# Attention in pairs of steps: both scores, both sets of transposes, then two weighted-value products in a row

## The chip, the cores and the metric

The kernel runs on one core of one Trainium2 chip. What counts is the device time of one execution in microseconds (us), and runs of the kernel are compared by their median. The engines are PE (TensorE: matrix products and transposes), DVE (VectorE), ACT (ScalarE), POOL (GpSimd) and SP (SyncE, which issues the DMAs). In the rows, PEld stands for the loads of PE's weights, which run beside its products.

## The reference

Clustered attention, then two expert layers on its output. Only the attention is touched by the change.

```python
def _attn_ref(q, k, v, centroids):            # (2, 8, 768, 64), 16 centroids a head
    ...
    q_assign = np.argmax(np.einsum('bhsd,hcd->bhsc', q_n, c_n), axis=-1)
    k_assign = np.argmax(np.einsum('bhsd,hcd->bhsc', k_n, c_n), axis=-1)
    mask = q_assign[:, :, :, None] == k_assign[:, :, None, :]
    scores = scale * np.matmul(q, k.transpose(0, 1, 3, 2))
    scores = np.where(mask, scores, -1000000000.0)
    scores = scores - np.max(scores, axis=-1, keepdims=True)
    attn = np.exp(scores)
    attn = attn / (np.sum(attn, axis=-1, keepdims=True) + 1e-09)
    return np.matmul(attn, v).astype(np.float32)

def reference(**kwargs):
    ...
    x = np.ascontiguousarray(attn_out.transpose(0, 2, 1, 3)).reshape(B * S, H * D)
    x = _moe_ref(x=x, **moe_kwargs)           # x @ w_in, a rational function, @ w_out
    return _moe2_ref(x=x, **moe2_kwargs)      # silu(x @ w_gate) * (x @ w_val) @ w_out
```

## The kernel before

Attention works on head pairs: 2 batches of 4 pairs of heads, 8 in all. A head pair has two halves of 384 queries; a half has three blocks of 128 queries for each of its two heads. One block of one head is a **step**, so a half has 6 steps (`PER`), a head pair 12, and the whole stage 96 (`order`). `n` counts the steps.

A step passes through these functions:

- `scores` (L344, L346): four products into `s_ps`, 128 queries by 768 keys, in PSUM. The centroid mask is part of the second product. `s_ps` has 2 buffers.
- `maximum` (L354): DVE takes the row maxima, into `st`.
- `exponentials` (L362): ACT makes `p` and the row sums. `p` has 3 buffers.
- `transposes` (L400), `LAG` = 2 steps later: PE transposes the six 128x128 blocks of `p` in two groups of three, each into a tile `t_ps`; each tile is copied to `pt` by ACT (L405), or in the second group of the steps in `dve_evac` by DVE (L403). The pool of `t_ps` has 3 buffers, which `r_ps` and `sim` share.
- `weighted` (L411): one of the six key blocks of a half that is finished: for each head one product of `v` and `pt`, summed up in `o_ps`, which has one buffer. The six are queued in `pv` once a half's last transposes stand in the program.

Each half also needs the reciprocals of its row sums: `reciprocals` (L369, L372, DVE), `spread` (L377: PE transposes them into `r_ps`; L379: ACT copies them; L381: a DMA to DRAM), `bring_back` (L388: a DMA back, broadcast over partitions into `rb`). When the sixth `weighted` of a half is there, `normalised` (L419, DVE) multiplies `o_ps` by `rb`, and `split_x` (L433, L434, POOL) splits the result for the expert layers.

`background` places other work between the steps: for the next head pair the centroid products `sims` (L277, PE), the search for the nearest centroid on DVE (`to_tokens` L284, `largest` L298, `reached` L303, `weigh` L309, `first_reached` L312, `one_hot` L315, `mask_values` L321, `to_rows` L329), and the split of the heads' q and k on POOL (L249 to L268); from step 60 on also nine weight blocks for the expert layers (L70 on ACT, L79 and L83 on DVE, L89 and L94 on POOL).

The order is written by hand: every engine runs its own instructions in the order in which the Python code makes them, and waits at the head of its queue for what an instruction needs. The loop from L540 on sets it, one step at a time:

```python
    for n in range(len(order) + LAG):
        s = n % (2 * PER)
        if n < len(order):
            scores(*order[n])
            maximum(*order[n])
```

After the loop `tail` does the last half's `weighted` in the first two rounds of the expert layers.

Of the kernel before, what the change touches and what calls it, by code (L numbers as in the profile page):

```python
# [20 lines left out]
def tile_kernel(ctx, tc, q_t, k_t, q_s, k_s, v_l, cent, w_in, w_out, a_co, b_co, w_gate, w_val, w_o2, out):  # L21
# [128 lines left out]
    order = [(b, hp, half, i, e) for b, hp in pairs for half in range(2) for i in range(HB) for e in range(2)]  # L150
    PER = 2 * HB
# [186 lines left out]
    def scores(b, hp, half, i, e):  # L338
        t = heads[b, 2 * hp + e]
        s_ps = ps_s.tile([P, S], F32, tag="s", name="s_ps")  # L340
        q0 = half * HALF + i * P
        qs = slice(q0, q0 + P)
        for lo, hi in CUT:
            nc.tensor.matmul(s_ps[:, lo:hi], t["q1"][:, qs], t["k1"][:, lo:hi], start=True, stop=False)  # L344
        for lo, hi in CUT:
            nc.tensor.matmul(s_ps[:, lo:hi], t["q2"][0:KM, qs], t["k2"][0:KM, lo:hi], start=False, stop=True)  # L346
        if (i, e) == (0, 0):
            live["st", b, hp, half] = st_p.tile([P, 3, PER], F32, tag="st", name="st")
        live["s", b, hp, half, i, e] = s_ps

    def maximum(b, hp, half, i, e):
        st = live["st", b, hp, half]
        k = e * HB + i
        nc.vector.tensor_reduce(  # L354
            out=st[:, 0, k:k + 1], in_=live["s", b, hp, half, i, e], axis=AX.X, op=ALU.max, negate=True
        )
# [33 lines left out]
    def transposes(b, hp, half, i, e, on_dve):  # L390
        p = live.pop(("p", b, hp, half, i, e))
        if i == 0:
            live["pt", b, hp, half, e] = pt_p.tile([P, NB, HALF], F32, tag="pt", name="pt")
        pt = live["pt", b, hp, half, e]
        qc = slice(i * P, (i + 1) * P)
        for g in range(2):
            t_ps = t_tile("t_ps")
            for j in range(HB):
                kb = g * HB + j
                nc.tensor.transpose(t_ps[:, j, :], p[:, kb * P:(kb + 1) * P], ident)  # L400
            ks = slice(g * HB, (g + 1) * HB)
            if g == 1 and on_dve:
                nc.vector.tensor_copy(out=pt[:, ks, qc], in_=t_ps)  # L403
            else:
                nc.scalar.copy(out=pt[:, ks, qc], in_=t_ps)  # L405
# [77 lines left out]
    dve_evac = (2, 8, 10, 11)  # L483
    n_early, every = 9, 4
    early0 = 60
    XS, BB = 3, 4
# [50 lines left out]
                    load_qk(b, 2 * hp + 1)  # L537

    LAG = 2
    for n in range(len(order) + LAG):  # L540
        s = n % (2 * PER)
        if n < len(order):
            scores(*order[n])
            maximum(*order[n])
        finished = None
        if pv:
            step = pv.pop(0)
            weighted(*step)
            if step[3] == NB - 1:
                finished = step[:3]  # L550
        if n >= LAG:
            transposes(*order[n - LAG], s in dve_evac)
        if n < len(order):
            exponentials(*order[n])
        if n % PER == 0 and n:
            reciprocals(*order[n - 1][:3])
        if n % PER == 1 and n > 1:
            spread(*order[n - 2][:3])
        if n % PER == BB and n > PER:
            bring_back(*order[n - BB - 1][:3])  # L560
        for engine in ("dma", "pe", "dve", "pool", "act"):
            background(n, engine)
        if finished:
            normalised(*finished)
            split_x(*finished)
        if n >= LAG and (n - LAG) % PER == PER - 1:
            pv.extend([order[n - LAG][:3] + (kb,) for kb in range(NB)])
# [269 lines left out]
```

## Time and profile before

| | us |
|---|---|
| median of 3 runs | 844.63 |
| lowest and highest | 844.25, 846.31 |
| the profiled execution | 844.0 |
| its span, from first to last instruction | 842.2 |

The rows further down come from one profiled execution. Their times start at the first instruction; each row of a timeline merges neighbouring instructions of one kind. `idle before <-releaser` in square brackets is how long the engine had been idle and what ended that; "issue" is idle time for which the profile shows no wait. The ends of matrix products are modelled, so starts are read here. Attention is the first 260 us of the span, the expert layers are the rest.

### The profile page before, as it was taken

Reading aid. Unit: us, or ns where it says so; the run is one execution under the profiler, and the core shown is the slowest. Engines: PE = TensorE matmul, PEld = TensorE weight load, DVE = VectorE, ACT = ScalarE, POOL = GpSimd, SP = SyncE. Lnnn points to the kernel's source line nnn. Section 1 sums busy time; section 2 is a strip of 40 time slices with the busy share of each in tenths; the row PEclk is TensorE's granted clock in tenths of the full one; section 3 lists DMA queues with packets and bytes.
Section 4 is the critical chain, followed back from the end, with each engine's and each line's share of the span. In section 5 each row is a group of like instructions: output and inputs, shape, how many; then the busy total and the mean of one; then the engine's idle time right before and its main releaser. Section 6 shows DMA issues by size and latency. Waiting matters only on the chain.

```text
span 842.2 us, 11048 instructions
## 1 busy us (share of the span) xinstructions
PE 807.8 (96%) x3900; PEld 606.0 (72%) x3900; DVE 621.3 (74%) x929; ACT 450.1 (53%) x850; POOL 311.9 (37%) x274
## 2 busy tenths in 40 slices
PE   4999999999899999999999989999999999999998
PEld 3665566555466887777777767788888888888886
DVE  7776687677765999999999999985576555434435
ACT  5666776666486897667667666842432222211111
POOL 3566375465532333433333433321244323211112
PEclk8899999999899999999999999999999999999999
DMA  5255335435222211111111211122223121100004
GB/s 179 83 174 168 112 87 169 148 117 172 76 87 90 75 51 59 68 50 51 51 50 55 72 50 51 51 75 76 75 90 104 57 75 50 51 26 1 0 1 149
DMA packets 26550, 67.90 MB, mean 81 GB/s; under 512 B 4448, under 2 KB 9536, under 8 KB 26496
## 3 DMA queue, kind: packets, MB, share of 16 engines
q1 hardware_dynamic: 26496, 67.21, 24.4%
q8 instruction: 30, 0.49, 0.2%
q14 instruction: 24, 0.20, 0.1%
HBM read 59.48 MB, written 3.19 MB: 74 GB/s over the span
## 4 chain that ended last, share of the span: by engine, by line
PE 70%; DVE 22%; issue 3%; ACT 2%; POOL 1%; DMA 1%; SPq 0%; DVEq 0%; POOLq 0%; ACTq 0%
PE h_ps L601 29%; PE acc L677 17%; PE o_ps L411 8%; PE t_ps L400 8%; PE s_ps L344 4%; PE s_ps L346 3%; DVE g L634 3%; DVE part L695 3%; DVE td L640 3%; DVE td L637 2%; DVE tq L620 2%; DVE tp L623 2%; DVE c L79 1%; DVE c L83 1%; DVE st L354 1%
## 5 line engine op out<-in xcount | busy, mean ns | idle before, releaser
L601 PE MATMUL h_ps<-yhl,w 128*128 128x512 f32 x864 | 201.8, 389 | 0.0
L601 PEld LDWEIGHTS h_ps<-yhl,w 128*128 128x128 f32 x864 | 162.2, 188 | 33.7
L677 PE MATMUL acc<-g,w 128*128 128x512 f32 x576 | 144.9, 395 | 11.5 <-DVE part L695 6.8
L601 PE MATMUL h_ps<-xhl,w 128*128 128x512 f32 x576 | 138.8, 390 | 0.0
L677 PEld LDWEIGHTS acc<-g,w 128*128 128x128 f32 x576 | 106.2, 188 | 42.2 <-DVE part L695 10.8
L94 POOL TENSOR_TENSOR w<-c,w 128x512 fp32r<-128x512 f32 x68 | 92.9, 1368 | 108.5 <-ACT w L91 101.4
L601 PEld LDWEIGHTS h_ps<-xhl,w 128*128 128x128 f32 x576 | 107.9, 188 | 23.9 <-issue 1.2
L645 POOL TENSOR_TENSOR g<-td,tr 128x512 fp32r<-128x512 f32 x46 | 59.6, 1295 | 172.7 <-DVE td L640 151.8
L354 DVE TENSOR_REDUCE st<-s_ps 128x1 f32<-128x768 f32 x96 | 91.3, 952 | 32.1 <-PE s_ps L346 29.3
L405 ACT COPY pt<-t_ps 128x384 f32<-128x384 f32 x160 | 70.4, 482 | 68.7 <-PE t_ps L400 68.5
L695 DVE TENSOR_TENSOR part<-acc,part 128x512 f32<-128x512 f32 x74 | 48.6, 685 | 75.3 <-PE acc L677 75.2
L400 PEld LDWEIGHTS t_ps<-ident,p 128*128 128x128 f32 x576 | 63.5, 144 | 55.7 <-issue 42.1
L677 PE MATMUL acc<-w,g 128*128 128x512 f32 x432 | 103.3, 389 | 0.0
L362 ACT ACTIVATE p<-s_ps,st 128x768 f32<-128x768 f32 x96 | 87.5, 912 | 11.3 <-DVE st L354 8.1
L677 PEld LDWEIGHTS acc<-w,g 128*128 128x128 f32 x432 | 81.1, 188 | 16.8
L411 PE MATMUL o_ps<-pt,v 128*64 128x384 f32 x384 | 84.1, 519 | 3.6 <-DVE x L419 3.6
L400 PE MATMUL t_ps<-ident,p 128*128 128x128 f32 x576 | 86.0, 287 | 0.0
L692 ACT COPY ts<-acc 128x512 f32<-128x512 f32 x22 | 12.9, 588 | 111.4 <-PE acc L677 111.4
L693 POOL TENSOR_TENSOR part<-ts,part 128x512 f32<-128x512 f32 x22 | 30.3, 1394 | 111.9 <-ACT ts L692 111.8
L618 ACT ACTIVATE tq<-h_ps,babs 128x512 f32<-128x512 f32 x48 | 33.0, 688 | 68.9 <-PE h_ps L601 66.6
L344 PE MATMUL s_ps<-k,q 128*128 128x512 f32 x192 | 59.7, 393 | 2.8 <-ACT p L362 2.7
L83 DVE SCALAR_TENSOR_TENSOR c<-raw,c 128x512 uint32<-128x512 uint32 x68 | 57.2, 841 | 2.0
(101 smaller groups left out, 1049.4 us busy)
## 6 DMA issues: line engine op xcount, KB each, us to landing
raw<-w_in_dram SPq DMA_DIRECT2D x16, 512.0 KB, 3.6
raw<-w_out_dram SPq DMA_DIRECT2D x16, 512.0 KB, 3.3
raw<-w_gate_dram SPq DMA_DIRECT2D x12, 512.0 KB, 3.3
raw<-w_val_dram SPq DMA_DIRECT2D x12, 512.0 KB, 3.3
raw<-w_o_dram SPq DMA_DIRECT2D x12, 512.0 KB, 3.3
xq<-q_t_dram SPq DMA_DIRECT2D x14, 384.0 KB, 4.6
xk<-k_t_dram SPq DMA_DIRECT2D x14, 384.0 KB, 6.4
sq<-q_s_dram SPq DMA_DIRECT2D x8, 384.0 KB, 3.0
```

The costliest lines, as they stand in the source:

```text
L83: nc.vector.scalar_tensor_tensor(out=cb, in0=t["low"].bitcast(U32), scalar=29, in1=cb, op0=ALU.logical_shift_right, op1=ALU.bitwise_or)
L94: nc.gpsimd.tensor_tensor(out=w[:, 1, :], in0=t["c"], in1=r32(w[:, 0, :]), op=ALU.subtract)
L344: nc.tensor.matmul(s_ps[:, lo:hi], t["q1"][:, qs], t["k1"][:, lo:hi], start=True, stop=False)
L354: nc.vector.tensor_reduce(out=st[:, 0, k:k + 1], in_=live["s", b, hp, half, i, e], axis=AX.X, op=ALU.max, negate=True)
L362: nc.scalar.activation(out=p, in_=live.pop(("s", b, hp, half, i, e)), func=AF.Exp, bias=st[:, 0, k:k + 1], accum_out=st[:, 1, k:k + 1],)
L400: nc.tensor.transpose(t_ps[:, j, :], p[:, kb * P:(kb + 1) * P], ident)
L405: nc.scalar.copy(out=pt[:, ks, qc], in_=t_ps)
L411: nc.tensor.matmul(live["o", b, hp, half][e * D:(e + 1) * D, :], heads[b, 2 * hp + e]["v"][:, kb, :], live["pt", b, hp, half, e][:, kb, :] ...
L601: nc.tensor.matmul(h_ps, w[:, wi, cs], x[:, xi, cc, :], start=(n == 0), stop=(n == 3 * NCC - 1))
L645: spread.tensor_tensor(out=g[:, 1, :], in0=td, in1=tr, op=ALU.mult)
L677: nc.tensor.matmul(acc[c], lhs, rhs, start=(first and m == 0), stop=(last and m == 2))
L695: nc.vector.tensor_tensor(out=pt[:, c, :], in0=banks[c], in1=pt[:, c, :], op=ALU.add)
```

## The change

The loop takes two steps at a time. In a pair it emits both `scores` and both `maximum`, the transposes of the first of the two steps that are due, both `exponentials`, the transposes of the second, then (where a half has ended) `reciprocals` and `spread` together, then two `weighted` in a row, then the background of both steps. `spread` used to stand in the step after `reciprocals`. The buffers, `LAG`, the copies' engines and the queue `pv` are as before.

```diff
     LAG = 2
-    for n in range(len(order) + LAG):
-        s = n % (2 * PER)
-        if n < len(order):
-            scores(*order[n])
-            maximum(*order[n])
-        finished = None
+    def next_weighted():
         if pv:
             step = pv.pop(0)
             weighted(*step)
             if step[3] == NB - 1:
-                finished = step[:3]
-        if n >= LAG:
-            transposes(*order[n - LAG], s in dve_evac)
-        if n < len(order):
-            exponentials(*order[n])
-        if n % PER == 0 and n:
-            reciprocals(*order[n - 1][:3])
-        if n % PER == 1 and n > 1:
-            spread(*order[n - 2][:3])
-        if n % PER == BB and n > PER:
-            bring_back(*order[n - BB - 1][:3])
-        for engine in ("dma", "pe", "dve", "pool", "act"):
-            background(n, engine)
+                return step[:3]
+
+
+    for n0 in range(0, len(order) + LAG, 2):
+        for n in (n0, n0 + 1):
+            if n < len(order):
+                scores(*order[n])
+                maximum(*order[n])
+        m0, m1 = n0 < len(order), n0 >= LAG
+        if m1:
+            transposes(*order[n0 - LAG], n0 % (2 * PER) in dve_evac)
+        if m0:
+            exponentials(*order[n0])
+            exponentials(*order[n0 + 1])
+        if m1:
+            transposes(*order[n0 + 1 - LAG], (n0 + 1) % (2 * PER) in dve_evac)
+        if n0 % PER == 0 and n0:
+            reciprocals(*order[n0 - 1][:3])
+            spread(*order[n0 - 1][:3])
+        finished = next_weighted()
+        finished = next_weighted() or finished
+        for n in (n0, n0 + 1):
+            if n % PER == BB and n > PER:
+                bring_back(*order[n - BB - 1][:3])
+            for engine in ("dma", "pe", "dve", "pool", "act"):
+                background(n, engine)
         if finished:
             normalised(*finished)
             split_x(*finished)
```

On PE, two steps in the middle of a half stand like this in the kernel before (one row for each group of like instructions; k and q have the numbers of the two heads):

```order
L344 MATMUL s_ps<-k_294,q_292 128x512
L344 MATMUL s_ps<-k_294,q_292 128x256
L346 MATMUL s_ps<-k_295,q_293 128x512
L346 MATMUL s_ps<-k_295,q_293 128x256
L411 MATMUL o_ps<-pt,v 64x384 x2
L400 MATMUL t_ps<-ident,p 128x128 x6
L344 MATMUL s_ps<-k_383,q_381 128x512
L344 MATMUL s_ps<-k_383,q_381 128x256
L346 MATMUL s_ps<-k_384,q_382 128x512
L346 MATMUL s_ps<-k_384,q_382 128x256
L411 MATMUL o_ps<-pt,v 64x384 x2
L400 MATMUL t_ps<-ident,p 128x128 x6
```

And like this in the changed kernel:

```order
L344 MATMUL s_ps<-k_302,q_300 128x512
L344 MATMUL s_ps<-k_302,q_300 128x256
L346 MATMUL s_ps<-k_303,q_301 128x512
L346 MATMUL s_ps<-k_303,q_301 128x256
L344 MATMUL s_ps<-k_401,q_399 128x512
L344 MATMUL s_ps<-k_401,q_399 128x256
L346 MATMUL s_ps<-k_402,q_400 128x512
L346 MATMUL s_ps<-k_402,q_400 128x256
L400 MATMUL t_ps<-ident,p 128x128 x12
L411 MATMUL o_ps<-pt,v 64x384 x4
```

The same instructions stand there; each kind is now in one block of twice the length, and the weighted products come last.

On DVE, around the middle of a head pair, from the maxima of steps 4 and 5 to those of step 7 and `normalised`, before:

```order
L354 TENSOR_REDUCE st<-s_ps 128x1
L312 TENSOR_REDUCE mx<-sm 128x24
L354 TENSOR_REDUCE st<-s_ps 128x1
L315 TENSOR_TENSOR sm<-wt,mx 128x384
L321 TENSOR_SCALAR sm<-sm,msk 128x384
L354 TENSOR_REDUCE st<-s_ps 128x1
L369 TENSOR_SCALAR st<-st 128x6
L372 RECIPROCAL st<-st 128x6
L329 STREAM_TRANSPOSE t_768<-sm 128x384
L354 TENSOR_REDUCE st<-s_ps 128x1
L419 TENSOR_TENSOR x<-o_ps,rb 128x384
```

And in the changed kernel:

```order
L354 TENSOR_REDUCE st<-s_ps 128x1 x2
L312 TENSOR_REDUCE mx<-sm 128x24
L315 TENSOR_TENSOR sm<-wt,mx 128x384
L321 TENSOR_SCALAR sm<-sm,msk 128x384
L354 TENSOR_REDUCE st<-s_ps 128x1 x2
L369 TENSOR_SCALAR st<-st 128x6
L372 RECIPROCAL st<-st 128x6
L329 STREAM_TRANSPOSE t_794<-sm 128x384
L419 TENSOR_TENSOR x<-o_ps,rb 128x384
```

The maxima stand in twos, the background work of both steps between them, and the reciprocals (L369, L372) stand behind two maxima instead of one.

On PE, where a half ends and a new head pair begins, before (the transpose of the reciprocals, L377, follows one step later, behind that step's transposes):

```order
L411 MATMUL o_ps<-pt,v 64x384 x2
L400 MATMUL t_ps<-ident,p 128x128 x6
L277 MATMUL sim<-sq,ct 32x384 x2
L277 MATMUL sim<-sk,ct 32x384 x2
L344 MATMUL s_ps<-k_717,q_715 128x512
```

And in the changed kernel:

```order
L400 MATMUL t_ps<-ident,p 128x128 x12
L377 MATMUL r_ps<-ident,st 6x128
L411 MATMUL o_ps<-pt,v 64x384 x4
L277 MATMUL sim<-sq,ct 32x384 x2
L277 MATMUL sim<-sk,ct 32x384 x2
L344 MATMUL s_ps<-k_626,q_624 128x512
```

L377 now stands in the same pair as the reciprocals and ahead of its weighted products, and the centroid products stand behind these instead of behind the transposes.

## Rows read from the trace of the kernel before

**Rows 1.** Stretch, length; busy us (count) PE, PEld, DVE, ACT, POOL; PE clock, DMA, GB/s.

```profile
45.97:74.95 28.98, 28.98 (x182) 17.34 (x178) 21.37 (x30) 19.83 (x47) 17.10 (x17) 1.00 0.51 166
...
132.70:161.56 28.86, 28.86 (x182) 17.32 (x178) 20.46 (x30) 19.74 (x47) 16.95 (x17) 1.00 0.48 155
161.56:195.66 34.10, 31.07 (x183) 18.42 (x179) 26.44 (x36) 21.63 (x50) 21.43 (x22) 0.95 0.39 124
195.66:231.47 35.81, 31.04 (x175) 18.43 (x171) 27.41 (x36) 20.55 (x48) 22.25 (x22) 0.90 0.38 122
```

**Rows 2.** Timeline of weight loads (PEld), one quiet step; columns: start, length, what.

```profile
84.27 0.30 PEld L344 LDWEIGHTS s_ps<-k,q 128*128 128x128 f32 x2
...
85.18 0.20 PEld L411 LDWEIGHTS o_ps<-pt,v 128*64 128x64 f32 x4 [0.25 <-issue]
85.97 0.64 PEld L400 LDWEIGHTS t_ps<-ident,p 128*128 128x128 f32 x6 [0.60 <-issue]
86.58 0.30 PEld L344 LDWEIGHTS s_ps<-k,q 128*128 128x128 f32 x2
```

**Rows 3.** Timeline of weight loads, three weighted products in a row in the tail.

```profile
263.32 0.20 PEld L411 LDWEIGHTS o_ps<-pt,v 128*64 128x64 f32 x4 [0.35 <-issue]
...
265.41 0.76 PEld L601 LDWEIGHTS h_ps<-xhl,w 128*128 128x128 f32 x4 [0.60 <-issue]
```

**Rows 4.** Timeline of weight loads, first head pair, steps without weighted products.

```profile
27.72 0.30 PEld L344 LDWEIGHTS s_ps<-k,q 128*128 128x128 f32 x2 [0.33 <-ACT p L362]
...
28.41 0.70 PEld L400 LDWEIGHTS t_ps<-ident,p 128*128 128x128 f32 x6
...
29.36 0.30 PEld L344 LDWEIGHTS s_ps<-k,q 128*128 128x128 f32 x2 [0.25 <-ACT p L362]
```

**Rows 5.** Timeline of weight loads, transposes with centroid products behind them.

```profile
102.23 0.64 PEld L400 LDWEIGHTS t_ps<-ident,p 128*128 128x128 f32 x6 [0.60 <-issue]
103.03 0.11 PEld L277 LDWEIGHTS sim<-sq,ct 128*32 128x32 f32 x2 [0.17 <-DVE st L372]
```

**Rows 6.** Timeline of the other engines in the step of rows 2, and later.

```profile
84.25 0.86 ACT L405 COPY pt<-t_ps 128x384 f32<-128x384 f32 x2 [0.55 <-PE t_ps L400]
...
85.00 0.92 ACT L362 ACTIVATE p<-s_ps,st 128x768 f32<-128x768 f32 x1
...
85.28 0.96 DVE L354 TENSOR_REDUCE st<-s_ps 128x1 f32<-128x768 f32 x1 [0.87 <-PE s_ps L346]
...
86.56 0.86 ACT L405 COPY pt<-t_ps 128x384 f32<-128x384 f32 x2 [0.55 <-PE t_ps L400]
...
205.94 0.19 ACT L362 ACTIVATION_READ_ACCUMULATOR p<-s_ps,st 128x1 f32 x1
...
206.18 0.30 PEld L344 LDWEIGHTS s_ps<-k,q 128*128 128x128 f32 x2 [1.18 <-ACT p L362]
```

**Rows 7.** The reciprocals: timelines at two places, then line L369 in sum (ns).

```profile
32.44 0.19 DVE L372 RECIPROCAL st<-st 128x6 f32<-128x6 f32 x1
...
32.74 0.08 PEld L377 LDWEIGHTS r_ps<-ident,st 128*6 128x6 f32 x1 [0.35 <-issue]
...
87.83 0.94 DVE L354 TENSOR_REDUCE st<-s_ps 128x1 f32<-128x768 f32 x1
88.69 0.93 DVE L369 TENSOR_SCALAR st<-st 128x6 f32<-128x6 f32 x1
...
L369 DVE TENSOR_SCALAR st<-st x16: 154/160/939, 32.2 to 258.4; 128x6 f32<-128x6 f32 x16
```

**Rows 8.** Timeline of PE near the start, transposes that keep it at work.

```profile
7.20 3.93 PE L198 MATMUL w_ps<-ident 128*128 128x128 f32 x27
```

**Rows 9.** Busy time by stretch, columns as in rows 1, where the clock differs.

```profile
8.79:12.00 3.21, 2.69 (x23) 2.37 (x21) 3.21 (x7) 2.01 (x4) 2.75 (x2) 1.00 0.27 61
...
212.50:217.00 4.50, 1.83 (x13) 1.26 (x11) 4.46 (x7) 1.74 (x4) 3.71 (x4) 1.00 0.20 44
217.00:223.83 6.83, 5.67 (x18) 2.88 (x18) 3.79 (x6) 3.06 (x7) 4.52 (x5) 0.50 0.37 108
```

## Prediction

> **What bounds the kernel now.** The change touches only the attention stage, which ends at about 260 us; the expert layers behind it keep their code, and I count them as unchanged. I first cut that stage by head pair, that is by 12 steps, from the score of step 12k+1 to the same score of the next head pair, with the view of busy time by stretches [rows 1]. Four head pairs take 28.86 to 28.98 us each (the first and the last of them are shown); PE is busy for all of that time at clock 1.00, DVE for about 21 us and ACT for 20. So PE sets the end there. The next two (34.10 and 35.81 us) are different: DVE has 26 to 27 us of work, PE is idle for 3 and 5 us, and the mean clock is below 1.
>
> Then I read one step on PE by its weight loads, since a load starts when PE turns to the next kind of work [rows 2]. Call the four score products S, the six transposes T and the two weighted-value products W. S lasts 0.91 us until W loads, W 0.79 until T loads, T 0.61 until the next S: 2.31 a step, 4.62 for two. The reader is to see the idle time with no releaser ("issue") before W and before T, which S behind T does not have: these are turns of PE, not waits.
>
> **The change part by part.**
>
> *Fewer turns of PE.* What each kind lasts when its own kind follows can be read elsewhere in the trace. S with T behind it lasts 0.69 [rows 4]. Three W in a row, in the tail, last 2.09, so (2.09 - 0.79) / 2 = 0.65 for a W with a W behind it [rows 3]. A T that comes after S spreads its six loads over 0.70 instead of 0.64, so it lasts 0.67 [rows 2, 4]. T with a differently shaped product behind it lasts 0.80 instead of 0.61, so 0.19 more [rows 5]. The new pair S S T T W W is then 0.69 + 0.69 + 0.67 + 0.67 + 0.19 + 0.65 + 0.79 = 4.35 us. Against 4.62 that saves 0.27 a pair, some 12 us over the 44 pairs that have W, if PE never waits.
>
> *A fourth transpose tile.* A pair writes four t_ps tiles and the pool has three, so the fourth waits for the copy of the first. Count from the pair's first S load: the T loads begin at 1.38. From T's first load to the first copy a step takes 0.59 [rows 2, 6], 0.65 with the slower loads; the copy takes 0.48, and PE goes on 0.05 after ACT is done (205.94 + 0.19 to 206.18) [rows 6]. The tile is free at 1.38 + 0.65 + 0.48 + 0.05 = 2.56. PE wants it one and a half T later, at 1.38 + 0.67 + 0.33 = 2.38. So 0.18 is lost, and a pair is 4.53. No row shows this wait itself. Its bounds are 0 (the copy ends in time) and 0.5 (one more copy of ACT ahead of it); I take 0.18, because each part of it has a row. That leaves 0.09 saved a pair.
>
> *ACT and the score buffers.* ACT copies the first two tiles from 2.03 on (the two take 0.75), then does both exponentials at 2.78 and 3.70 (0.92 each), then two more copies at 4.62 [rows 6]. The score buffers come free some 0.14 after an exponential's end, at 3.84 and 4.76; the next pair wants them at 4.53 and 5.22. So both waits are hidden by about 0.5, and DVE's maxima may start about 1.3 late before PE feels it. If that cover goes, each further us of lateness is one on PE.
>
> *The reciprocals, moved next to their transpose.* Before, DVE did L369 and L372 in one step and PE transposed the result (L377) at the end of the next one. Now both stand in the pair that starts a half, and L377 stands ahead of W W on PE. The first maximum starts 1.00 after S's load [rows 2, 6], the second 0.86 later, L369 0.86 after that [rows 7], at 2.72, L372 0.20 later; it ends at 3.11, and PE loads L377 0.11 after that [rows 7], at 3.22. PE is there at 2.89. So 0.33 is lost, twice a head pair; L377 itself costs 0.1 as before. With the turn and W W such a pair is 4.89. L369 also has two lengths, 0.16 and 0.93 [rows 7]; four of its 16 were long, all in the middle of a head pair, where GpSimd prepares the next heads. That was covered by a step; now 0.77 would go straight onto PE. It hit four of the seven middles that have such GpSimd work: 0.44 a head pair.
>
> *The centroid products (sims)* move behind W W, where they wait for the third copy (4.62 + 0.48 + 0.05 = 5.15 against 4.89) but save the turn behind T (0.19). They took 28.9 - 12 x 2.31 - 2 x 0.1 = 0.98 and I leave them at that. DVE stands idle with to_tokens at the head of its queue until they are done, so the maxima of the next pair start about 0.6 late, which is within the 1.3. The normalised product, which L411 waited for in the busy head pairs, gets a whole pair more time.
>
> *The sum.* A quiet head pair: 4 x 4.53 + 2 x 4.89 + 0.98 + 0.44 = 29.3 against 28.9, so 0.4 slower; I add 0.15 for lateness that DVE carries into the middle pair. Four of them: +2.2. In the first head pair W is missing and the pair goes round the chain S, T, copies, two exponentials: 0.69 + 0.65 + 0.75 + 1.84 + 0.2 = 4.13 against two steps of 1.64 [rows 4]: +0.85, for the one pair that this holds. The last 12 steps have no preparation for a next head: -0.1.
>
> *The two busy head pairs* also prepare weight blocks on DVE. I walked DVE through them with the lengths that its operations had there before. In the first three pairs of each it has 5 to 6 us of work for a pair of 4.5, and in the first of them it idles for sims. By the middle pair its maxima are some 3 us late; 1.3 of that is covered, and then L377 waits for all that is left. This makes 4.4 and 5.6 us of delay, and behind waits of that length PE falls to half its clock for a stretch [rows 9], which I put at 1.1 us each. After: 2 x 28.86 + 4.4 + 5.6 + 2.2 = 69.9. Before: 34.10 + 35.81 [rows 1] and the 0.98 of the sims that stand just ahead, 70.9. So -1.0, with 3 us either way.
>
> Total: 0.85 + 2.2 - 1.0 - 0.1 = +2.0 us. The profiled execution took 844.0 (span 842.2), so 846.0. It lies 0.6 below the median of the runs shown (844.63), and I forecast 846.5.
>
> **The rivals.** *PE's saving survives (faster).* If the fourth tile's wait is near its lower bound and L369 stays short, a quiet head pair is 4 x 4.35 + 2 x 4.89 + 0.98 = 28.2, 0.7 faster; over six head pairs that is -4. If the busy ones, which stand 12 us above two quiet ones [rows 1], lose a third of that too, it is -8: 837 to 841. For it: PE is the bound, and every term of the saving has a row. Against it: each new wait is worked out from rows as well.
>
> *DVE's lateness lands on L377 (slower).* In the middle pair of a head pair L377 waits for everything that DVE still has to do. If L369 is long there and the operations before it too, since they share their cause, DVE is 1 to 2 us late in the quiet head pairs also. It decides from a lateness of 0.2 on, as nothing covers L377 any more. At 1 us for each of the six or seven, and one more stretch at half clock (2 us), the time is 846.5 + 8 to 9, so 852 to 856. For it: the 0.93 row. Against it: DVE is busy for only 21 of 29 us there [rows 1].
>
> *The clock falls among the transposes (slower).* In rows 9 PE fell to half its clock (1.2 GHz) behind a stretch in which it was busy for 1.83 of 4.50 us. The new pair has 12 transposes and a wait in a row, about 1.7 of 4.5 us. If that made it fall once in each half, for half the 6.83 us of rows 9, of which about half is lost, 15 halves are some 25 us: 870. Against it: at the start PE did 27 transposes in a row [rows 8], and the clock behind their first part was 1.00 [rows 9]. The Trainium skill's page "TensorE: Matmul & The Clock Gate" (Part 4) says that transposes do not count as busy for the clock as other matmuls do; by that rule the fall would come. The trace speaks mostly against it here.
>
> **How the numbers follow.** Forecast 0.43 (846.5, by itself 843 to 850), saving survives 0.27, DVE onto L377 0.26, clock 0.04. About 0.3% (2.5 us, so 842.1 to 847.2 is "the same") is what a measurement of this kernel can tell from no change. The forecast's case gives 0.03 faster, 0.28 same, 0.12 slower; the first rival 0.23 faster and 0.04 same; the second 0.02 same and 0.24 slower; the clock 0.04 slower. Faster 0.26, same 0.34, slower 0.40. The range takes in the upper part of the fast rival and most of the slow one: 839.5 to 855.
>
> **What would show it.** In the new profile PE's loads in a quiet pair should read 0.69 and 0.69 for the scores, then 12 transposes with an idle time of about 0.2 before the tenth that ACT's copy ends, then W W in 1.44; pairs should start 4.5 apart. L377 should wait for L372 by 0.3, or by 1.1 where L369 is long. If pairs are 4.35 apart, the tile term was wrong; if L377 does not wait, the reciprocal term was. I am wrong altogether if PE waits for ACT's exponentials in quiet pairs, or if the two busy head pairs move by more than 3 us.

## The result, and the profile after

The changed kernel took **854.49 us** (median of 4 runs, 852.39 to 855.76) against 844.44 for the kernel before beside it (4 runs): a ratio of **1.0117**, 95% interval 1.0084 to 1.015. It is about 10 us slower. The time lies near the upper end of the range, and where the second rival, "DVE's lateness lands on L377", put it (852 to 856), not at the forecast of 846.5. The profiled execution of the changed kernel took 855.41, its span 853.6, 11.4 more than the span before.

First the busy time by head pair, cut at the first score load of each head pair's first step. The columns are the stretch, its length, busy time of PE, weight loads, DVE, ACT and POOL, granted clock, DMA share and GB/s, as in [rows 1]. The kernel before, cut the same way: a quiet head pair and the two busy ones.

```profile
100.53:129.41 28.88, 28.88 (x180) 17.34 (x179) 21.84 (x30) 19.73 (x47) 16.28 (x16) 1.00 0.43 132
158.27:192.37 34.10, 31.07 (x181) 18.42 (x180) 26.42 (x36) 21.63 (x50) 20.72 (x22) 0.95 0.40 134
192.37:229.13 36.76, 31.99 (x180) 18.59 (x179) 27.40 (x37) 21.50 (x50) 22.24 (x23) 0.91 0.40 124
```

The changed kernel, the same three head pairs and the stretch at half clock in the first busy one:

```profile
104.46:134.87 30.41, 28.44 (x180) 18.53 (x178) 21.56 (x30) 19.31 (x47) 16.27 (x16) 1.00 0.41 124
165.28:202.29 37.01, 31.68 (x180) 20.02 (x178) 24.56 (x36) 20.95 (x50) 20.44 (x20) 0.91 0.39 126
202.29:239.96 37.67, 31.30 (x180) 19.91 (x178) 26.29 (x37) 21.14 (x50) 22.13 (x22) 0.91 0.38 121
...
188.20:195.00 6.80, 6.17 (x19) 3.58 (x20) 3.16 (x8) 2.16 (x7) 5.15 (x5) 0.50 0.33 96
```

PE's work in a quiet head pair did fall, from 28.88 to 28.44. But where it had no idle time before, it now idles for 2.0 us, and 30.41 is the sum. By the starts of the head pairs in both traces the 11.4 us are: the start-up ahead of the first score +1.5 (the code there is the same; the clock reached 1.00 at 10.70 us, where it had at 8.79), the first head pair -0.5, four quiet ones +6.0, the two busy ones +3.8, the last +0.7, the expert layers -0.1.

What PE waited for is in the view of its waits (us in total, times, longest). Two lines of the changed kernel:

```profile
PE r_ps L377 <- DVE st L372: 18.9, 8, 5.1
...
PE s_ps L344 <- ACT p L362: 3.0, 4, 1.0
```

All eight of these waits of L377 are in the middle of a head pair, one in each. In the kernel before L377 waited twice, both times in a busy head pair: 1.0 us for L372 and 1.9 for an exponential.

A normal pair, by its weight loads (start, length, what, idle time before it and its releaser), to hold against [rows 2]:

```profile
84.44 0.30 PEld L344 LDWEIGHTS s_ps<-k,q 128*128 128x128 f32 x2 [0.60 <-issue]
...
85.83 1.02 PEld L400 LDWEIGHTS t_ps<-ident,p 128*128 128x128 f32 x9
87.01 0.31 PEld L400 LDWEIGHTS t_ps<-ident,p 128*128 128x128 f32 x3 [0.15 <-ACT pt L405]
87.49 0.20 PEld L411 LDWEIGHTS o_ps<-pt,v 128*64 128x64 f32 x4 [0.17 <-issue]
...
88.93 0.30 PEld L344 LDWEIGHTS s_ps<-k,q 128*128 128x128 f32 x2 [0.60 <-ACT p L362]
```

From 84.44 to 88.93 are 4.49 us, where two steps before took 4.62. The break of 0.15 ahead of the last three of twelve transposes is the wait for the fourth tile.

The next pair is the middle of the head pair. DVE, GpSimd and PE there:

```profile
84.74 2.09 DVE L309 TENSOR_TENSOR sm<-sm,wt 128x384 f32<-128x384 f32 x1
...
89.06 1.71 DVE L315 TENSOR_TENSOR sm<-wt,mx 128x384 f32<-128x384 f32 x1
90.80 0.87 DVE L321 TENSOR_SCALAR sm<-sm,msk 128x384 f32<-128x384 f32 x1
91.59 1.80 DVE L354 TENSOR_REDUCE st<-s_ps 128x1 f32<-128x768 f32 x2
93.31 0.15 DVE L369 TENSOR_SCALAR st<-st 128x6 f32<-128x6 f32 x1
93.50 0.19 DVE L372 RECIPROCAL st<-st 128x6 f32<-128x6 f32 x1
...
84.38 2.03 POOL L268 TENSOR_TENSOR k<-xk,k 64x768 fp32r<-64x768 f32 x1
...
88.52 1.83 POOL L260 TENSOR_TENSOR q<-xq,q 64x768 fp32r<-64x768 f32 x1
...
93.84 0.27 PE L377 MATMUL r_ps<-ident,st 128*6 128x128 f32 x1 [1.71 <-DVE st L372]
```

Here L369 is short. What is long stands ahead of it: L309 and L315, of which the shortest of full size in the traces of all runs take 0.54 each, took 2.09 and 1.71. Each began while a GpSimd subtraction ran, and ended 0.4 us after it (86.41 and 86.83; 90.35 and 90.77). The maxima, which read PSUM, keep their 0.90 (1.80 for two). So DVE reaches L369 late, and L377 lets PE wait 1.71 with W W queued behind it.

The two lines over the whole attention stage (ns: shortest, median, longest), in the kernel before and then in the changed one, show that the new order makes them meet GpSimd more often:

```profile
L309 DVE TENSOR_TENSOR sm<-sm,wt x9: 351/1306/1977, 9.0 to 205.0; 128x384 f32<-128x384 f32 x7, 128x192 f32<-128x192 f32 x2
L315 DVE TENSOR_TENSOR sm<-wt,mx x9: 457/890/2173, 11.7 to 211.1; 128x384 f32<-128x384 f32 x7, 128x192 f32<-128x192 f32 x2
```

```profile
L309 DVE TENSOR_TENSOR sm<-sm,wt x9: 354/1983/2093, 10.2 to 215.6; 128x384 f32<-128x384 f32 x7, 128x192 f32<-128x192 f32 x2
L315 DVE TENSOR_TENSOR sm<-wt,mx x9: 456/1706/2153, 12.8 to 222.4; 128x384 f32<-128x384 f32 x7, 128x192 f32<-128x192 f32 x2
```

In the first busy head pair the middle looks like this (ACT, DVE, PE):

```profile
182.22 0.70 ACT L70 ACTIVATE u<-raw 128x512 f32<-128x512 f32 x1
...
183.03 0.66 DVE L79 TENSOR_SCALAR c<-u 128x512 uint32<-128x512 uint32 x1 [2.06 <-ACT u L70]
183.60 2.15 DVE L315 TENSOR_TENSOR sm<-wt,mx 128x384 f32<-128x384 f32 x1
...
188.83 0.37 PE L377 MATMUL r_ps<-ident,st 128*6 128x128 f32 x1 [4.76 <-DVE st L372]
```

DVE stands 2.06 us for ACT's block shift (L70), which is issued in the same pair as the bit operation that reads it (L79) and stands behind both exponentials and the copies on ACT. Then L315 takes 2.15, and L377 waits 4.76. At the end of that wait the clock falls to 0.50 of full speed, that is to 1.2 GHz, for 6.8 us, and the same in the second busy head pair. The kernel before had 3.4 and 6.8 us at 0.50 in these two.

### The profile page after: what moved, and what is told of

Read it like the earlier page. It is cut to its first block, busy times and chain, and to the rows that moved or that the text cites. A ratio compares the mean times of both kernels' runs of the same rounds, so it can differ in the third digit from the quotient of the medians.

```text
span 853.6 us, 11038 instructions
## 1 busy us (share of the span) xinstructions
PE 805.1 (94%) x3900; PEld 614.9 (72%) x3900; DVE 619.6 (73%) x929; ACT 446.4 (52%) x850; POOL 312.0 (37%) x274
## 4 chain that ended last, share of the span: by engine, by line
PE 58%; DVE 31%; issue 4%; ACT 3%; SPq 1%; POOL 1%; DMA 1%; DVEq 0%; ACTq 0%; POOLq 0%
PE h_ps L609 28%; PE acc L685 16%; PE o_ps L411 5%; DVE st L354 5%; PE t_ps L400 3%; DVE g L642 3%; DVE part L703 3%; PE s_ps L344 3%; DVE td L648 3%; DVE td L645 3%; DVE tq L628 2%; DVE tp L631 2%; PE s_ps L346 2%; DVE sm L315 2%; DVE sm L309 1%
## 5 line engine op out<-in xcount | busy, mean ns | idle before, releaser
L685 PE MATMUL acc<-g,w 128*128 128x512 f32 x576 | 145.0, 395 | 11.5 <-DVE part L703 6.7
L405 ACT COPY pt<-t_ps 128x384 f32<-128x384 f32 x160 | 70.4, 487 | 74.8 <-PE t_ps L400 74.7
L354 DVE TENSOR_REDUCE st<-s_ps 128x1 f32<-128x768 f32 x96 | 87.6, 949 | 26.8 <-PE s_ps L346 26.6
L400 PE MATMUL t_ps<-ident,p 128*128 128x128 f32 x576 | 78.0, 279 | 0.0
L411 PE MATMUL o_ps<-pt,v 128*64 128x384 f32 x384 | 74.9, 514 | 0.0
L344 PE MATMUL s_ps<-k,q 128*128 128x512 f32 x192 | 57.5, 382 | 3.0 <-ACT p L362 3.0
L83 DVE SCALAR_TENSOR_TENSOR c<-raw,c 128x512 uint32<-128x512 uint32 x68 | 56.8, 836 | 2.0
```

What stands on the lines that cost most here:

```text
L83: nc.vector.scalar_tensor_tensor(out=cb, in0=t["low"].bitcast(U32), scalar=29, in1=cb, op0=ALU.logical_shift_right, op1=ALU.bitwise_or)
L354: nc.vector.tensor_reduce(out=st[:, 0, k:k + 1], in_=live["s", b, hp, half, i, e], axis=AX.X, op=ALU.max, negate=True)
L411: nc.tensor.matmul(live["o", b, hp, half][e * D:(e + 1) * D, :], heads[b, 2 * hp + e]["v"][:, kb, :], live["pt", b, hp, half, e][:, kb, :] ...
L685: nc.tensor.matmul(acc[c], lhs, rhs, start=(first and m == 0), stop=(last and m == 2))
```

## The experiments

The theory after the result: the loss is DVE's lateness, and it shows at L377 because nothing lies between the reciprocals and their transpose any more, nor between that and W W. Three things could be undone: the distance, the cover on PE, and the cause of the lateness.

**The distance given back: L377 one pair later.**

```
-            spread(*order[n0 - 1][:3])
+        if n0 % PER == 2 and n0 > 2:
+            spread(*order[n0 - 3][:3])
...
+    spread(*order[-1][:3])
```

> The changed kernel with one part undone: the transpose of the reciprocals (L377) goes back to a later place, one pair after the reciprocals, behind that pair's transposes. Theory (L377 stands right behind DVE's late work and ahead of the weighted products, and PE pays the lateness in full): the 18.9 us that PE waited at L377 vanish, a quiet head pair falls from 30.4 to about 28.2 us, and the total to 836 to 842 us. Rival (DVE is the bound in the middle pair, and L377 is only where it shows): the wait moves to the score buffers (PE waiting for ACT's exponentials, which wait for DVE's maxima), and the total stays above 849.

Measured: 848.6 us (median of 5), ratio to before 1.0062 (1.0041 to 1.0083). No L377 waits for L372 now, and three of the quiet head pairs are 29.43 (the other 30.60). But a new wait stands there, 14 times, 10.9 us in all:

```profile
112.33 0.55 DVE L403 COPY pt<-t_ps 128x384 f32<-128x384 f32 x1
...
112.93 0.27 PE L377 MATMUL r_ps<-ident,st 128*6 128x128 f32 x1 [0.93 <-DVE pt L403]
```

L377 writes a transpose tile, and the buffer that it gets there is one that DVE has to copy out first (L403), behind its maxima. It is DVE's lateness again, by another way. In the two busy head pairs the scores now wait 2.46 and 2.83 us for exponentials, the place that the rival named; the time lies between the two forecasts. By the ratios the distance is worth some 5 us of the 10, and L377 has no free place one pair on.

**The distance taken from the kernel before**, one part of the change alone:

```
-        if n % PER == 1 and n > 1:
-            spread(*order[n - 2][:3])
+            spread(*order[n - 1][:3])
```

> The kernel before with one part of the change alone: L377 (spread) directly behind the reciprocals, in the same step, where it stood at the end of the next step. One step at a time otherwise. Theory (the lost distance between the reciprocals and L377 costs by itself): in a quiet middle L372 ends about 2.9 us after the step's first score load (86.9 to 89.85 in the trace of before) and PE comes to L377 after 2.2, so L377 waits 0.7 to 0.8 where L369 is long and under 0.1 where it is short; about 3 to 4 us in all with the busy middles, where DVE is later; the median 846 to 850. Rival (the scores two at a time are needed for DVE to be that late): L377 waits less than 0.2 in every quiet middle and the median is 843.5 to 845.

Measured: 849.51 (9 runs), ratio 1.0066 (1.0045 to 1.0088).

```profile
89.87 0.92 DVE L369 TENSOR_SCALAR st<-st 128x6 f32<-128x6 f32 x1
...
91.16 0.27 PE L377 MATMUL r_ps<-ident,st 128*6 128x128 f32 x1 [0.84 <-DVE st L372]
```

L377 waits 0.84 in three of the quiet middles and 1.48 in the fourth, 0.88 in the first head pair and 3.3 and 3.7 in the busy ones (the 1.48 and the 3.7 end with an exponential, whose sums the reciprocals take). So moving the transpose next to its reciprocals costs over 5 us by itself, with one score at a time as well.

**The reciprocals ahead of the pair's two maxima.**

```
+        if n0 % PER == 0 and n0:
+            reciprocals(*order[n0 - 1][:3])
         for n in (n0, n0 + 1):
             if n < len(order):
                 scores(*order[n])
                 maximum(*order[n])
```

> The changed kernel with the reciprocals (L369, L372) put ahead of the pair's two maxima on DVE; L377 stays in that pair ahead of the weighted products. Theory (two maxima ahead of L369, 1.7 us, are what makes L377 late): in a quiet middle pair L372 ends 1.7 us earlier, the wait of 1.7 goes, head pairs take about 28.3 to 28.8, total 842 to 846. Rival (the lateness stems from the pairs ahead and only shifts: the maxima now come later by the reciprocals): gain under 3 us, total above 851.

Measured: 848.04 (9 runs), ratio 1.0048 (1.0031 to 1.0065). Quiet head pairs fell from 30.4 to between 28.46 and 28.96, about as long as those of the kernel before (28.86 to 28.99), and L377 does not wait in them. That is what the theory said of them; the time lies above its 842 to 846, because of the other head pairs. The busy ones still took 34.3 and 37.6, and there L377 waits 3.80 and 5.44; the first:

```profile
183.86 0.27 PE L377 MATMUL r_ps<-ident,st 128*6 128x128 f32 x1 [3.80 <-DVE st L372]
```

The first head pair took 35.2 where it had taken 31.3: another 6.8 us at half clock, from 34.7 on, behind a wait of 0.99 of L377 and within one of 1.56 of the scores, which ended at 35.4. So two maxima of cover (1.8 us) are enough against the quiet pairs' lateness and not against the busy ones'.

**One DVE operation fewer.** The one-hot step of the mask (L315) is left out for the later heads, so their mask is incomplete:

```
-[first_reached], [one_hot, mask_values]]
+[first_reached], [mask_values]]
```

> The changed kernel with one_hot (L315, DVE) left out for every head pair but the first, so part of the mask is not computed. In the changed kernel L315 takes 1.7 us in the pair ahead of the middle pair, where it needs 0.55 alone, since GpSimd works at the same time. Theory (the wait at L377 is what DVE is late): the middle pair's maxima are on time, the wait at L377 falls from 1.7 to about 0.3 us in the quiet head pairs and by some 2 us in each of the two busy ones; total about 845 us. Rival (the wait belongs to the place alone, whatever DVE does before): it stays at 1.3 us or more, and the total above 851.

Measured: 852.61 (one run). With 1.71 us of DVE's queue gone, the wait of L377 fell only from 1.71 to 1.41 in three of the four quiet middles (in the first from 1.34 to 0.36), and in the busy ones from 4.76 to 3.66 and not at all (5.08, now 5.26). One of the three:

```profile
86.97 1.50 DVE L321 TENSOR_SCALAR sm<-sm,msk 128x384 f32<-128x384 f32 x1
...
90.12 0.97 DVE L369 TENSOR_SCALAR st<-st 128x6 f32<-128x6 f32 x1
...
86.43 1.82 POOL L260 TENSOR_TENSOR q<-xq,q 64x768 fp32r<-64x768 f32 x1
...
89.26 1.80 POOL L268 TENSOR_TENSOR k<-xk,k 64x768 fp32r<-64x768 f32 x1
```

By the numbers the rival held, though not for its reason: L321 now meets the GpSimd subtraction that L315 had met, and goes from 0.87 to 1.50; L369 meets the next one, ends at 91.09 with it (91.06), and is 0.97 long. The sum of DVE's work is not what is late here; whichever of these operations meets GpSimd is.

**GpSimd's subtractions made short.** L260 and L268 become one-input operations of the same size; this kernel leaves out the low parts of the later heads' q and k.

```
-nc.gpsimd.tensor_tensor(out=t["q1"][D:P, :], in0=t["xq"][D:P, :], in1=r32(t["q1"][D:P, :]), op=ALU.subtract)
+nc.gpsimd.tensor_scalar(out=t["q1"][D:P, :], in0=t["xq"][D:P, :], scalar1=1.0, scalar2=0.0, ...)
```

(and the same for `k2` in k_lo)

> The changed kernel in which GpSimd's two subtractions for the next heads (q_lo L260 and k_lo L268, TENSOR_TENSOR of 1.83 and 2.03 us) are TENSOR_SCALAR copies of the same size, with the same output and without the second input; the low parts of the later heads are left out by this, so the scores lose their correction. Theory (a DVE operation on SBUF that starts while GpSimd works there ends only some 0.3 us after GpSimd's, and this is what L377 waits for in the quiet head pairs): a TENSOR_SCALAR of this size takes 0.83, so four times a head pair GpSimd is done 1.0 to 1.2 us earlier, and its work for the next heads ends at about 88.5 where it ended at 93.3, ahead of one_hot, mask_values and L369. L309 falls from 2.09 to about 1.0, L315 from 1.71 to 0.6, L369 is 0.16 everywhere; the 1.3 to 1.7 us that L377 waits in quiet middles fall to under 0.4; quiet head pairs 29.0 to 29.3 where they were 30.40; the median 845 to 849. Rival (DVE is late by its own work and by the order of its queue, the GpSimd operations beside it only happen to lie there): L377 keeps at least 1.2 us, head pairs stay above 30.1, the median above 852.

Measured: 843.9 (10 runs, 839.31 to 846.46), ratio 0.9989 (0.9963 to 1.0015). From L309 on, lines are 4 higher in this kernel. L309 and L315, the reciprocal step, and a quiet head pair:

```profile
81.92 1.07 DVE L313 TENSOR_TENSOR sm<-sm,wt 128x384 f32<-128x384 f32 x1
...
85.22 0.70 DVE L319 TENSOR_TENSOR sm<-wt,mx 128x384 f32<-128x384 f32 x1
...
88.56 0.16 DVE L373 TENSOR_SCALAR st<-st 128x6 f32<-128x6 f32 x1
...
99.73:128.49 28.76, 28.35 (x180) 18.54 (x178) 19.61 (x30) 19.10 (x47) 12.45 (x16) 1.00 0.42 132
```

Nothing was taken from DVE's or PE's queue, and DVE's busy time fell by 2 us a quiet head pair all the same. L377 waits only once in the quiet head pairs, by 0.29, and the middle pair takes 4.91 in three of them. So the time that DVE loses beside GpSimd is the cause there. The median is even below the theory's 845 to 849. By the medians it is as large as the whole loss of the change: the changed kernel without it takes what the kernel before takes with it. The kernel before was not run with the short subtractions, so how much that one would gain stays open. (The profiled execution, 839.3, was the lowest of the ten times, so I read the waits from it and the time from the median.) The busy middles keep waits of 3.3 and 4.2.

**The bit operations of the weight blocks one step later**, a pair behind ACT's shift:

```
-            elif engine == "dve" and r == 1:
+            elif engine == "dve" and r == 2:
                 block_bits_1(started[j])
-            elif engine == "dve" and r == 2:
+            elif engine == "dve" and r == 3:
                 block_bits_2(started[j])
```

> The changed kernel with DVE's two bit operations of each weight block one step later (block_bits_1 at r = 2, block_bits_2 at r = 3), so that ACT's block_shift, which is issued at r = 0, is a whole pair ahead of them. Theory (in the busy head pairs DVE idles 2.06 us at the head of its queue for ACT's shift, which stands behind both exponentials and the copies of the same pair, and all of it reaches L377): the idle time in front of L79 goes, L377 in the two busy middles falls from 4.76 and 5.08 to about 2.5 to 3.5, the busy head pairs from 37.01 and 37.67 to 34.5 to 36; quiet ones stay at 30.4; the median 849 to 852. Rival (DVE's sheer amount of work in those pairs is what is late): L377 keeps over 4.3 in both and the median stays at 853 to 856.

Measured: 846.43 (10 runs), ratio 1.0027 (1.0004 to 1.005). DVE does not stand for L70 any more:

```profile
184.76 0.37 PE L377 MATMUL r_ps<-ident,st 128*6 128x128 f32 x1 [2.48 <-DVE st L372]
...
164.29:196.87 32.58, 29.83 (x181) 18.89 (x179) 24.54 (x36) 21.05 (x50) 20.04 (x20) 0.95 0.47 148
```

L377 waits 2.48 and 2.27 where it had 4.76 and 5.08, and the stretch at half clock is 3.4 us instead of 6.8 in both busy head pairs. They took 32.58 and 33.96, 8.1 us less in sum, a larger gain than either theory had: 5.1 of it is the wait, and 3.0 is PE's busy time (29.83 and 30.19 against 31.68 and 31.30), which the clock gave back. The last head pair, which also prepares weight blocks, gained too: its middle went from 5.83 to 4.91.

**Cover on PE: W W between the two sets of transposes** (S S T W W T). L377 stays where it is in the code, and so lands behind the last T.

```
+        finished = next_weighted()
+        finished = next_weighted() or finished
         if m1:
             transposes(*order[n0 + 1 - LAG], (n0 + 1) % (2 * PER) in dve_evac)
         if n0 % PER == 0 and n0:
             reciprocals(*order[n0 - 1][:3])
             spread(*order[n0 - 1][:3])
-        finished = next_weighted()
-        finished = next_weighted() or finished
```

> The changed kernel with the two weighted products moved between the two sets of transposes (S S T W W T instead of S S T T W W); all else, the reciprocals next to their transpose L377 too, stays. L377 then stands behind the pair's last transposes, where PE comes to it some 1.4 us later in the pair. Theory (the fourth transpose tile waits for ACT's copy, and L377 costs what of DVE's lateness the products ahead of it on PE don't cover): the weighted products give ACT the time to copy, so no L400 waits for ACT in a pair; S S 1.38, T 0.86 with the turn behind it, W W 1.44, T 0.64 make pairs of 4.3 to 4.4 where they were 4.49; the wait of L377 in quiet middles falls from 1.3 to 1.7 us to 0 to 0.4; quiet head pairs 27.2 to 28.0, the median 828 to 838. Rival (ACT's copies and exponentials are what is late, and will be wherever the tiles stand): the wait goes from L400 to the scores' L344, which wait for the exponentials; pairs stay at 4.45 or above and the median above 842.

Measured: 837.87 (5 runs), ratio 0.9928 (0.9899 to 0.9957): by the ratios some 16 us less than the changed kernel. The middle pair of a quiet head pair, by weight loads, with DVE's reciprocal:

```profile
86.89 0.30 PEld L344 LDWEIGHTS s_ps<-k,q 128*128 128x128 f32 x2
...
88.29 0.70 PEld L400 LDWEIGHTS t_ps<-ident,p 128*128 128x128 f32 x6
89.15 0.20 PEld L411 LDWEIGHTS o_ps<-pt,v 128*64 128x64 f32 x4 [0.17 <-issue]
...
90.59 0.64 PEld L400 LDWEIGHTS t_ps<-ident,p 128*128 128x128 f32 x6 [0.60 <-issue]
91.20 0.09 PEld L377 LDWEIGHTS r_ps<-ident,st 128*6 128x6 f32 x1
91.31 0.30 PEld L344 LDWEIGHTS s_ps<-k,q 128*128 128x128 f32 x2
...
90.85 0.19 DVE L372 RECIPROCAL st<-st 128x6 f32<-128x6 f32 x1
```

L369 was long here too (0.98), L372 ended at 91.04, and PE came to L377 at 91.20 without a wait. Normal pairs are 4.31, with no break in the transposes: the fourth tile's wait is gone with the same move, and T with S behind it needs no turn. Quiet head pairs take 27.57 in three of four (29.01 in the first); the busy ones take 30.80 and 36.17, and L377 still waits 2.56 and 4.11 in them.

**Only the weighted products two at a time**, in the kernel before: two in every second step, behind its transposes, in place of one in each step ahead of them. Scores, transposes and reciprocals stay one step at a time:

```
+        for _ in range(2 if n % 2 else 0):
+            if pv:
...
```

> The kernel before with one part of the change alone: the weighted products two at a time, in every second step behind its transposes; scores, maxima, exponentials and reciprocals stay single as before. Theory (the saving is two turns of PE per two steps, and all that lost time was the rest of the pairing): two steps take 4.35 us instead of 4.62, a quiet head pair 27.4 instead of 28.9 us, the whole 830 to 835 us. Rival (the turns save nothing of the whole because PE then waits for DVE and ACT, who have 21 of 27 us to do): 840 to 845.

Measured: 832.36 (4 runs), ratio **0.9866** (0.9837 to 0.9895). Two steps take 4.38 and a quiet head pair 27.25. The part of the change that pays is this one, and it needs no fourth tile and no short distance.

**That kernel with the bit operations one step later** (the edit above):

> The kernel before with the weighted products two at a time on odd steps (as in the run with that alone, 832.4 us) and with DVE's two bit operations of each weight block one step later. There no reciprocal's transpose stands close, and the two busy head pairs (33.63 and 34.52 us against 27.25 for a quiet one) lose their time in scores that wait for ACT's exponentials, which wait for DVE's maxima. Theory (what the later bit operations gave in the changed kernel was the wait for ACT's shift, in front of which DVE stood): here DVE idles only 0.45 us at that place, so little is to be had: busy head pairs 32.5 to 34.5, the median 830 to 833. Rival (the later place is better because the bit operations then miss GpSimd's work): the busy head pairs fall by 1.5 us or more each, to under 32.5, and the median is 826 to 829.5.

Measured: **827.48** (4 runs), ratio 0.9812 (0.9774 to 0.985). The busy head pairs without the edit, then with it:

```profile
151.60:185.23 33.63, 29.43 (x180) 19.18 (x178) 27.69 (x36) 20.96 (x49) 21.51 (x22) 0.95 0.47 145
185.23:219.75 34.52, 29.41 (x180) 19.53 (x178) 28.14 (x37) 21.54 (x50) 22.27 (x23) 0.95 0.40 132
```

```profile
152.36:182.58 30.22, 28.22 (x180) 18.68 (x178) 24.70 (x36) 21.67 (x50) 20.96 (x20) 1.00 0.48 156
182.58:214.67 32.09, 28.42 (x180) 18.65 (x179) 25.01 (x37) 21.50 (x50) 22.60 (x22) 1.00 0.45 142
```

Here the rival held. DVE hardly stood for ACT's shift, but its busy time fell by 3 us in each head pair with the same operations: L79 and L83, the bit operations, take 10.6 us in the two head pairs where they took 14.6. That they meet less of GpSimd's work at the later place is my reading of it. The clock stayed at 1.00. This is the lowest median of the study.

**S S T W W T with the later bit operations**, and then with sims directly behind W W as well:

> S S T W W T (837.9 us as run before) with DVE's two bit operations of each weight block one step later. Quiet head pairs stay at 27.57. Theory (the two causes of L377's wait in the busy middles, DVE's stand for ACT's shift and the missing cover on PE, add up): L377's waits of 2.56 and 4.11 fall to 0 to 1.5, no stretch at half clock follows them, the busy head pairs fall from 30.80 and 36.17 to 29 to 32; the median 830 to 835. Rival (with the cover there, the shift no longer matters, and the busy pairs are bound by DVE's amount of work): they stay within 1 us in sum, the median 836 to 839.

> The kernel of the run before this one (S S T W W T, bit operations later) with the centroid products (sims) directly behind W W, ahead of the pair's second transposes, where they stood at its end and waited 0.42 us for ACT's copy of a transpose tile. Theory: W W gives ACT the time for that copy, the wait goes and one turn with it; the pairs with sims go from 5.89 to 5.3 to 5.5, quiet head pairs from 27.57 to 27.0 to 27.2; 2 to 3 us less than that run in all. Rival (sims take a transpose tile, and the second set of transposes then waits for the copy instead): pairs with sims stay at 5.8 or above, and the median is within 1 us of that run's.

Measured: 831.43 (ratio 0.9863, 0.9837 to 0.9889) and 828.76 (0.9837, 0.9803 to 0.9872). In the first the busy head pairs took 29.95 and 32.03, as expected. In the second the pair with sims fell from 5.89 to 5.30 and a quiet head pair to 26.98, the shortest of all, as the theory said; the medians are 2.7 us apart, but the two intervals overlap. It stands level with the kernel of 827.48: some 2 us more in the first head pair (32.2 against 30.3) use up what it gains in the quiet and the busy ones.

## Why the prediction was right or wrong

The range held the time; the forecast's case did not come, the second rival did. Of the 11.4 us between the spans the sum had +2.0. That the time fell into the rival's 852 to 856 is in part luck: 1.5 us more of start-up and 1.8 us less for the clock in the first head pair (below), neither of them in any sum, nearly cancel.

- *Fewer turns, and the fourth tile*: right. The pair was put at 4.53 and is 4.49; the wait, put at 0.18 with bounds of 0 and 0.5, is 0.15. The order S S T W W T shows it from the other side, since there both go.
- *Score buffers, sims, the pair that ends a half*: right. 4.89 + 0.98 = 5.87 was the sum, 5.88 is the row, and in quiet head pairs no score waits for ACT.
- *L377 behind the reciprocals*: the mechanism was right and the size was wrong. The middle of a quiet head pair was put at 4.89 + 0.44 + 0.15 = 5.48 and is 6.55 in three of four: 1.07 too little, and the whole 3.8 us by which the four were missed. The step that failed is the term for lateness, "it hit four of the seven middles that have such GpSimd work: 0.44 a head pair", with 0.15 for all else. I took L369's two lengths as a matter of L369. In the trace it is one of several: L303, L309, L315 and L321, and L79 and L83 in the busy head pairs, are long in the same way when they start while GpSimd works. Not every DVE operation on SBUF is (lines further down). In three of the four quiet middles of the changed kernel L369 itself was short, and L309 and L315 ahead of it had taken 2.7 us more than their shortest. Where neither meets GpSimd for long (the run with short subtractions) the middle is 4.91, as the 4.89 without lateness said. So the price per event was in [rows 7], but it had to be looked for in every DVE operation ahead of L369 that can be held so. The 4.89 itself is slightly off its terms (PE there at 2.89, 0.33, 0.1 for L377, the turn of 0.19, W W in 1.44), which add up to 4.95; where no sims follow, the trace has 4.91.
- *The tolerance of 1.3 us*: right for scores, but it does not apply to L377, and that was in the text. It is the reason that DVE, at 21.6 of 30.4 us busy, sets the time.
- *The busy head pairs*: L377's waits were put at 4.4 and 5.6 and are 4.76 and 5.08. What failed is the price of the clock behind them, 1.1 us each. PE's busy time is 31.68 and 31.30 there against 28.44 in a quiet head pair, 3.2 and 2.9 more. Those 3.9 us and 1.3 of waits for exponentials (0.27 and 1.03), which the sum did not have, are the difference between its 69.9 and the 74.7 in the trace, but for 0.4. The kernel before had most of the clock's cost too (31.07 and 31.99 of PE's busy time), so against it the loss of 3.8 is idle time.
- *The first head pair*: put at +0.85, measured -0.5. A pair without W is 3.85, where 4.13 was the estimate, against 3.37 before; so the cost was there, under another gain. PE's busy time in that head pair fell by 1.8 us (25.59 to 23.78): near its beginning 6.8 us ran at half clock (17.52 to 24.35), where before it was 10.2 (15.62 to 25.86). Other runs have either length with either order of the steps, so I take this for chance; no run here settles it.
- *The last 12 steps*: put at -0.1, measured +0.7. They have no next head to prepare, but they do prepare weight blocks, and L377 waits 1.06 in their middle too; with the bit operations one step later it does not.
- *The clock among transposes*: did not come. Quiet head pairs run at 1.00 with 12 transposes in a row. The Trainium skill's page "TensorE: Matmul & The Clock Gate" (Part 4) says that transposes do not count as busy for the clock in the same way. The traces speak against that: at the start the clock even rose to 1.00 among the 27 transposes that stand behind the first centroid products (at 8.79 us before [rows 8], at 10.70 in the changed kernel).
- *The first rival* (the saving survives, 837 to 841) would have come with cover on L377: S S T W W T gives 837.9.

What decided between forecast and rival was that several DVE operations share one cause. The text of the rival had that ("the operations before it too, since they share their cause") and held DVE's 21 of 29 us busy against it. That share was the wrong evidence: L377 asks when one operation ends, and the share of a head pair does not tell that.

The Trainium skill's page "SBUF — State Buffer" (section "SBUF: two separate sides") has the rule that fits: DVE and GpSimd share a pair of ports as an exclusive lock, held for a whole instruction, and a DVE operation needs it when it has two SBUF inputs (then against a GpSimd operation that reads SBUF) or runs in a two-port mode. The rows agree as far as they go: L309 and L315 (two inputs) and L321 and L369 (one input, SBUF to SBUF) are held until GpSimd's instruction is over, and the maxima from PSUM never are. Nor are L298, L312, L329 and L372, with one SBUF input each; two of them in the kernel before, at their usual length inside a subtraction:

```profile
60.18 0.19 DVE L372 RECIPROCAL st<-st 128x6 f32<-128x6 f32 x1
60.29 0.54 DVE L329 STREAM_TRANSPOSE t<-sm 128x384 f32<-128x384 f32 x1
...
59.99 1.84 POOL L260 TENSOR_TENSOR q<-xq,q 64x768 fp32r<-64x768 f32 x1
```

Whether L321 and L369 ran in a two-port mode, no row shows. That it is these ports, and not another shared thing, no run here shows.

Still open: how much of the 16 us of S S T W W T belongs to the tile and how much to the cover on L377 in the busy head pairs, since one edit moves both. In a quiet head pair it is 0.18 for each of four pairs (4.49 to 4.31; the one with sims stays at 5.88) and 2.1 for the middle.

## What to carry to other kernels

When a change shortens the bound engine's own work, list each instruction of that engine that reads another engine's result, and ask how late that result may come before and after; here a step of distance, or 1.4 us of work of its own between the two, was worth more than the turns it cost. The lateness to reckon with is not the producer's mean duration but that of its whole queue when all of it meets what can hold it: here the DVE operations of the mask (L303, L309, L315, L321) and L369 beside GpSimd's work. And try the part of a change that saves by itself: pairing the weighted products alone was worth 11.5 us, pairing everything cost 10.

## What the runs showed of the hardware

- A DVE operation with two SBUF inputs that takes 0.54 us at its shortest (L309, L315) took up to 2.15 when it started while a GpSimd operation ran on SBUF, and ended 0.4 us after it (90.35 and 90.77). L369, with one input of 128x6, goes from 0.16 to 0.98 and ended with it (91.06 and 91.09). Reductions from PSUM kept their 0.90 at the same time, and a stream transpose (0.54) and a reciprocal (0.19) on SBUF were not held.
- With GpSimd's subtractions 1 us shorter, DVE was 2 us less busy in a quiet head pair (21.56 to 19.61) with the same operations.
- A stretch of 6.8 us at clock 0.50 added 2.9 to 3.2 us to PE's busy time, one of 3.4 us 1.4 to 1.8. The length of the one wait ahead of it does not tell which comes: behind waits of 4.8 to 5.1 us it was 6.8 and behind 2.3 to 2.5 with the later bit operations 3.4, but with L377 one pair later 6.8 followed a wait of 2.46, and with the short subtractions the clock did not fall behind one of 3.27.
